# Attention and a Mish feed-forward on one core: the order of the seven-product blocks, attention by single tiles, PSUM banks as tiles of their own, sums on GpSimd

## The chip, the cores and the metric

The kernel runs on one core of a Trainium2 chip. The metric is the device time in microseconds (us), median of the runs shown. TensorE multiplies matrices into PSUM, VectorE and ScalarE read PSUM and work elementwise, GpSimd works on SBUF, SyncE issues transfers. Each engine takes its instructions in the order in which the program wrote them and waits on semaphores.

## What is computed

Attention inside chunks of 64 positions, then a feed-forward with Mish, all in float32:

```python
q_c = q.reshape(B, H, nc, chunk, D)          # B 8, H 8, S 576, chunk 64, D 64; k_c, v_c alike
scores = scale * np.matmul(q_c, k_c.transpose(0, 1, 2, 4, 3))
scores = scores - np.max(scores, axis=-1, keepdims=True)
attn = np.exp(scores)
attn = attn / (np.sum(attn, axis=-1, keepdims=True) + 1e-09)
out = np.matmul(attn, v_c)
...
x = np.ascontiguousarray(attn_out.transpose(0, 2, 1, 3)).reshape(B * S, H * D)   # 4608 x 512
h = x @ w_in                                  # 512 x 2048
sp = np.where(h > 20.0, h, np.log1p(np.exp(np.minimum(h, 20.0))))
g = h * np.tanh(sp)
return (g @ w_out).astype(np.float32)         # 2048 x 512
```

## The kernel before, in words

**Tiles.** The 4608 tokens are 36 attention tiles of 128 tokens (two chunks of 64). Every factor of the feed-forward is split into two parts of fewer bits, a rounded one and the residue ("hi" and "lo"), and a product is the sum of three matmuls: lo by hi, hi by lo, hi by hi. ScalarE writes the hi part (a cast), VectorE the lo part (a subtraction of two SBUF operands).

**First part: plain blocks.** Two blocks of 512 tokens (tiles 0 to 7) run in 32 "slots" (`slot(s)`), one for each block and each 128 columns of `w_in`: `up` of the next slot (12 matmuls), `down` of the last (12 matmuls into four accumulators `o_o`), the attention of tiles 4 to 7, and of tiles 8 to 15 (`AHEAD`, pairs 4 to 7), and the preparation of the weights. In slots 16 to 31 the weights of the second part are made: `t_sum` (two sums of 512 columns), `t_diff` (four differences of 256), `t_hi`, `t_lo`, once in two slots, and written to DRAM (`dwi`). After slot 31 come the down of the last slot and the store of the second block.

**Second part: seven-product blocks.** Tiles 8 to 35 are four blocks of seven tiles (896 tokens, in halves of 448 columns). The up projection is a two-by-two block product with seven products in place of eight (Strassen's, in Winograd's form), for pairs of 128 columns of `w_in`. Eight such pairs make eight "sets" for each block, 32 in all (set z is pair z mod 8 of block z div 8). In a set TensorE runs

- `s_up(z, k)`, k = 0 to 6 ("u0" to "u6"), six matmuls of 448 columns each. u0, u3, u5 and u6 accumulate in a bank `al` of that set, u1 in the first half of the tile `bg`, u2 and u4 in the second half. `s_copy` (ScalarE) keeps intermediate states p1 (after u0), p5 (after u2) and u2 (after u3). `s_c` (VectorE) adds them to the products: c11 after u1, c12 after u4, c22 after u5. `s_hi` (ScalarE: Mish and cast) and `s_lo` (VectorE) make g of the four quadrants 11, 12, 22 and 21 from them.
- `s_down(z-1, i)`, i = 0 to 6 ("d0" to "d6"), six matmuls of 512 columns each with the g of the set before, for the seven tiles of tokens. They alternate between the two halves (banks) of one tile `d`. `s_out` empties each: a copy on ScalarE in a block's first set, then a sum on VectorE into `sum0` to `sum6`, in the last set into a new tile `ob` (of three) that two transfers write to DRAM.

**Order.** The order of the second part is written by hand: `ORDER` gives fourteen places of a set, alternately u and d, with d5 and d6 next to each other and u6 last. `when(z, m, ...)` puts work of the other engines behind place m of set z, `pe[z, m]` work of TensorE.

**Attention in the second part.** `plan_pair` puts a pair of tiles into a set: scores at place 1, maximum and subtraction at 2, exponential at 4, sums and reciprocals at 5, normalisation at 7, transposes at 9, values at 12, the copy into x at 13. Ten pairs (8 to 17) have three, four and three sets of the first three blocks. `ps_a` is a tile of two banks for scores, transposes and values. With it PSUM is full: two banks in `ps_h`, two in `ps_a`, four in `ps_o`.

**x of the next block.** In a block's last set (z = 7, 15, 23) `plan_x` makes the seven operands `xo0` to `xo6` of the next block: four sums or differences of 896 elements (`x_sum`: xs and x, L553), seven casts (`x_hi`, ScalarE, L558), seven residues (`x_lo`, VectorE, L561), each behind the product that last reads its place. For the first block they are made before and after slot 30.

Line numbers in the profile of before: `up` L308, `down` L346, `store` L360 and L362, small matmuls of attention L180, transposes L251, `s_up` L602, `s_down` L621, `s_out` L646 (copy) and L649 (sum), `s_copy` L660, `s_c` L669, `s_hi` L681 (Mish) and L682 (cast), `s_lo` L685. A program line that stands for several helper calls keeps the helper's number.

Of the kernel before, what the change touches and what calls it, by code (L numbers as in the profile page):

```python
# [25 lines left out]
def kernel(  # L26
# [485 lines left out]
    cols = {}  # L512
    rows = [[] for _ in range(NSB)]
    for j in range(FIRST_TILE // 2, NPAIR):
        blocks = [(2 * j + t - FIRST_TILE) // BT for t in range(2)]
        parts = [(blocks[0], BOTH)] if blocks[0] == blocks[1] else [(blocks[t], slice(t, t + 1)) for t in range(2)]
        cols[j] = []
        for b, ts in parts:
            cols[j].append((b, len(rows[b]) * CHUNK, ts))
            rows[b] += [((2 * j + t) * 2 + c) * CHUNK for c in range(2) for t in range(ts.start, ts.stop)]  # L520
# [39 lines left out]
    def x_lo(b, k):  # L560
        nc.vector.tensor_tensor(  # L561
# [79 lines left out]
    def s_out(z, i):  # L641
        b, s = divmod(z, NS)
        o = places["d"][:, (BT * z + i) % 2]
# [289 lines left out]
```

## Time and profile before

| | us |
|---|---|
| median of 3 runs (lowest, highest) | 981.82 (980.07, 983.72) |
| the profiled execution itself | 984.02 |
| its span, first to last instruction | 982.2 |
| TensorE busy / VectorE / ScalarE / GpSimd in the span | 875.6 / 532.1 / 426.0 / 0.7 |
| mean granted TensorE clock | 0.974 |

A row of the timeline reads: start, duration, engine, line, operation, out<-in, partitions x elements, type, count; in brackets the idle time of that engine just before, and who released it. PE is TensorE's matmuls, PEld its loads of the stationary operand, DVE VectorE, ACT ScalarE, POOL GpSimd. A group's row has the busy time, the mean ns of one, and behind the second bar the idle time before the group with its main releaser. The first part lasts to about 225 us, set 0 to about 252, the last set's downs begin at 961.

### The profile page before, as it was taken

To read this page: it belongs to the slowest core of one execution; us is meant where nothing else is said; L and a number is where in the kernel's file an instruction comes from. 1 tells how busy PE (TensorE), PEld (TensorE's weight loads), DVE (VectorE), ACT (ScalarE), POOL (GpSimd) and SP (SyncE) were. 2 spreads that over 40 slices of the span, in tenths; PEclk is the share of its full clock that TensorE was granted. 3 is DMA by queue.
4 is the path that set the end of the run, shared out by engine and by line. 5 is a ranking of instruction groups with operands and counts; after the bars stand their busy time and mean duration, and the time that the engine had idled before them with its cause. 6 is when DMAs were issued, how large, how long until landed. Compare 5 with 4: busy or idle time off the path is not lost.

```text
span 982.2 us, 14424 instructions
## 1 busy us (share of the span) xinstructions
PE 875.6 (89%) x5984; PEld 719.2 (73%) x5984; DVE 532.1 (54%) x802; ACT 426.0 (43%) x669; POOL 0.7 (0%) x6
## 2 busy tenths in 40 slices
...
GB/s 258 253 324 369 307 220 158 139 100 263 211 175 143 171 174 148 85 215 225 150 174 115 227 113 43 220 183 196 91 234 133 129 60 229 129 129 160 183 43 75
DMA packets 51297, 170.81 MB, mean 174 GB/s; under 512 B 5152, under 2 KB 11296, under 8 KB 39968
## 3 DMA queue, kind: packets, MB, share of 16 engines
...
q10 hardware_dynamic: 848, 1.44, 0.4%
...
## 4 chain that ended last, share of the span: by engine, by line
PE 64%; DVE 16%; ACT 9%; DMA 5%; issue 5%; SPq 1%; POOLq 0%; DVEq 0%; ACTq 0%; POOL 0%
PE d L621 28%; PE al L602 14%; PE bg L602 8%; PE o_o L346 4%; PE h L308 3%; DVE sum L649 3%; DMA wos<-in_w_out 2%; DVE xo L561 2%; PE s L180 2%; DMA out<-ob 2%; DVE m L207 2%; PE av L180 2%; DVE c L669 2%; PE pt L251 2%; ACT c L681 1%
## 5 line engine op out<-in xcount | busy, mean ns | idle before, releaser
L621 PE MATMUL d<-wo,g 128*128 128x512 f32 x1344 | 362.1, 405 | 76.8 <-DVE sum L649 57.2
L621 PEld LDWEIGHTS d<-wo,g 128*128 128x128 f32 x1344 | 252.0, 191 | 148.9 <-DVE sum L649 74.5
L649 DVE TENSOR_TENSOR sum<-d,sum 128x512 f32<-128x512 f32 x168 | 115.6, 688 | 141.8 <-PE d L621 141.7
L602 PE MATMUL al<-xo,ring 128*128 128x448 f32 x768 | 179.2, 376 | 1.9 <-DVE c L669 1.9
L602 PEld LDWEIGHTS al<-xo,ring 128*128 128x128 f32 x768 | 148.4, 195 | 19.7 <-DVE c L669 2.3
L681 ACT ACTIVATE c<-c 128x448 f32<-128x448 f32 x96 | 55.5, 578 | 232.3 <-DVE c L669 232.2
L602 PE MATMUL bg<-xo,ring 128*128 128x448 f32 x576 | 137.4, 375 | 7.5 <-DVE c L669 7.5
L685 DVE TENSOR_TENSOR g<-c,g 128x448 fp32r<-128x448 f32 x128 | 79.3, 620 | 91.4 <-ACT g L682 91.4
L602 PEld LDWEIGHTS bg<-xo,ring 128*128 128x128 f32 x576 | 108.6, 191 | 25.5 <-DVE c L669 12.1
L308 PE MATMUL h<-x,w 128*128 128x512 f32 (+1 forms) x396 | 94.6, 389 | 0.8 <-ACT x L282 0.8
L308 PEld LDWEIGHTS h<-x,w 128*128 128x128 f32 x396 | 73.6, 192 | 15.8 <-ACT x L282 0.9
L346 PE MATMUL o_o<-w,gh 128*128 128x512 f32 x256 | 81.8, 402 | 0.0
L682 ACT CAST g<-c 128x448 fp32r<-128x448 f32 x128 | 72.5, 567 | 4.1
L346 PE MATMUL o_o<-w,gl 128*128 128x512 f32 x128 | 53.1, 415 | 6.1 <-DVE gl L333 6.1
L346 PEld LDWEIGHTS o_o<-w,gh 128*128 128x128 f32 x256 | 49.8, 195 | 10.3
L681 ACT ACTIVATE c<-al 128x448 f32<-128x448 f32 x32 | 17.4, 545 | 82.8 <-PE al L602 82.8
L561 DVE TENSOR_TENSOR xo<-x,xo 128x896 fp32r<-128x896 f32 x24 | 25.9, 1091 | 37.7 <-ACT xo L558 37.7
L660 ACT COPY u<-al 128x448 f32<-128x448 f32 x32 | 17.1, 534 | 57.2 <-PE al L602 57.0
L649 DVE TENSOR_TENSOR ob<-d,sum 128x512 f32<-128x512 f32 x28 | 19.3, 690 | 36.1 <-PE d L621 26.7
L669 DVE TENSOR_TENSOR c<-bg,u 128x448 f32<-128x448 f32 x32 | 20.0, 624 | 32.0 <-PE bg L602 32.0
L207 DVE TENSOR_REDUCE m<-s 128x16 f32<-128x1024 f32 (+1 forms) x20 | 22.3, 1117 | 23.5 <-PE s L180 23.4
L346 PEld LDWEIGHTS o_o<-w,gl 128*128 128x128 f32 x128 | 24.7, 193 | 12.7 <-DVE gl L333 7.5
...
## 6 DMA issues: line engine op xcount, KB each, us to landing
...
```

The lines of the kernel that those rows point to most:

```text
L180: nc.tensor.matmul(o[h * CHUNK : (h + 1) * CHUNK, c, t - ts.start, g], lhsT=l[rows, t, 2 * g + h], rhs=r[rows, t, 2 * g + h], start=True, ...
L207: nc.vector.tensor_reduce(out=small(j, "m", t), in_=st[j]["s", t.start].rearrange("p c t g k -> p c (t g) k"), op=ALU.max, axis=AX.X,)
L308: nc.tensor.matmul(h[:, cols], lhsT=wi(f, w_, kt), rhs=x[:, kt, cols], start=(n == 0), stop=(n == 3 * NK - 1),)
L346: nc.tensor.matmul(acc[t], lhsT=g[:, sl], rhs=w_part(f, w_), start=(f == 0 and n == 0), stop=(f == NF - 1 and n == 2),)
L561: nc.vector.tensor_tensor(out=xo[k][:, 1], in0=x_src(b, k), in1=raw(xo[k][:, 0]), op=ALU.subtract)
L602: nc.tensor.matmul(o[:, :HALF], lhsT=w_[:, wn, kt * P : (kt + 1) * P], rhs=x[:, xn, kt], start=(n == 0 and k < 3), stop=(n == 5), skip_gro ...
L621: nc.tensor.matmul(o, lhsT=g_tile(z, e)[:, gn, i * P : (i + 1) * P], rhs=wos[z % 2][:, e, wn], start=(n == 0), stop=(n == 5),)
L649: nc.vector.tensor_tensor(out=to, in0=o, in1=a, op=ALU.add)
L669: nc.vector.tensor_tensor(out=ct[z, n], in0=o[:, :HALF], in1=ct.pop((z, other)), op=ALU.add)
L681: nc.scalar.activation(out=ct[z, n], in_=src, func=AF.Mish)
L682: nc.scalar.copy(out=g_view(z, n, 0), in_=ct[z, n])
L685: nc.vector.tensor_tensor(out=g_view(z, n, 1), in0=ct.pop((z, n)), in1=raw(g_view(z, n, 0)), op=ALU.subtract)
```

## The change

- `ORDER` becomes u0, e6, u1, d0, u2, d1, ..., u6, d5: u and d strictly alternate. d0 to d5 are of the set before, e6 is d6 of the set two before. Two more rounds of `s_set` behind set 31 run the remaining downs.
- PSUM: after set 0 the pool of the first part is closed, and its four banks become four tiles `b`, `g`, `d0`, `d1`. u1 writes `b`, u2 and u4 write `g`, the downs alternate between `d0` and `d1`, and those of set 31 go round all four. In set 0, b and g are a tile of `ps_a`.
- Attention in the second part is planned by single tiles (`plan_tile`), one in each of the sets 1 to 6, 8 to 14 and 16 to 22: twenty in place of ten pairs. Scores, maximum and v at place 1, subtraction at 3, exponential at 4, sums at 7, normalisation at 8, transposes at 9, values at 13, the copy into x at place 0 of the next set. Columns of x follow tiles (`x_put`, `row`).
- Sums: `t_sum` and `t_diff` run on GpSimd; so do `x_sum` for blocks 1 to 3, and their residue `x_lo` of k = 2. The residues of k = 4, 5, 6 move to the next set, and `x_hi` from the even places to the odd ones behind them.
- `s_out` of a block's last set adds in the sum's own tile and writes it out from there.
- Passage to the second part: the downs of slots 30 and 31 are divided and lie at places 1, 3, 5 and 11 of set 0; residues and casts of the first x are spread differently; the ring of weights is loaded after slot 27.

The diff, cut:

```diff
-    ps_o = ctx.enter_context(tc.tile_pool(name="ps_o", bufs=1, space=bass.MemoryType.PSUM))
+    plain = ctx.enter_context(ExitStack())
+    ps_o = plain.enter_context(tc.tile_pool(name="ps_o", bufs=1, space=bass.MemoryType.PSUM))
...
-            nc.vector.tensor_tensor(
+            nc.gpsimd.tensor_tensor(
                 out=d[e], in0=raw(w_part(f, 0)), in1=raw(w_part(f, 1)), op=ALU.add
             )
...
-            nc.vector.tensor_tensor(out=o, in0=a, in1=b, op=ALU.subtract)
+            nc.gpsimd.tensor_tensor(out=o, in0=a, in1=b, op=ALU.subtract)
...
+    def n_scores(n):
+        qk = tl[n]["qk"]
+        small_mm(n_bank(n, "s"), qk[:, 0:1], qk[:, 1:2], slice(0, 1))
...
+    LOW_BY_POOL = (2,)
...
-        nc.vector.tensor_tensor(out=o, in0=l, in1=r, op=op)
+        engine = nc.gpsimd if b else nc.vector
+        engine.tensor_tensor(out=o, in0=l, in1=r, op=op)
...
     def x_lo(b, k):
-        nc.vector.tensor_tensor(
+        engine = nc.gpsimd if b and k in LOW_BY_POOL else nc.vector
+        engine.tensor_tensor(
...
-            places["bg"] = ps_o.tile([P, 2, DM], F32, name="bg", tag="o0")
+            o = ps_a.tile([P, 2, DM], F32, name="bg", tag="a")
+            places["b"], places["g"] = o[:, 0], o[:, 1]
...
-        o = places["bg"][:, int(k > 1)] if k in (1, 2, 4) else places["a", z]
+        o = places["b"] if k == 1 else places["g"] if k in (2, 4) else places["a", z]
...
+    def d_bank(z, i):
+        if z == NSB * NS - 1:
+            return places[("d0", "d1", "b", "g")[(BT * z + i) % 4]]
+        return places[f"d{(BT * z + i) % 2}"]
...
-        o = places["d"][:, (BT * z + i) % 2]
+        o = d_bank(z, i)
         a = s_sum(i)
...
-        to = a if s < NS - 1 else wst.tile([P, DM], F32, name=f"ob_{z}_{i}", tag="c")
-        nc.vector.tensor_tensor(out=to, in0=o, in1=a, op=ALU.add)
+        nc.vector.tensor_tensor(out=a, in0=o, in1=a, op=ALU.add)
...
-        if 1 <= s <= N:
+        if 1 <= s < N - 1:
             down(s - 1)
...
-    ORDER = (("u", 0), ("d", 0), ("u", 1), ("d", 1), ("u", 2), ("d", 2), ("u", 3), ("d", 3),
-             ("u", 4), ("d", 4), ("u", 5), ("d", 5), ("d", 6), ("u", 6))
+    ORDER = (("u", 0), ("e", 6), ("u", 1), ("d", 0), ("u", 2), ("d", 1), ("u", 3), ("d", 2),
+             ("u", 4), ("d", 3), ("u", 5), ("d", 4), ("u", 6), ("d", 5))
...
-        when(z, 13, lambda: s_hi(z, 21))
-        when(z + 1, 0, lambda: s_lo(z, 21))
...
+        when(z, 12, lambda: s_hi(z, 21))
+        when(z, 13, lambda: s_lo(z, 21))
...
-        when(z - 1, 13, lambda: x_sum(b, 2))
-        for k, m in enumerate((0, 2, 4, 6, 8, 10, 13)):
-            when(z, m, lambda k=k: x_hi(b, k), lambda k=k: x_lo(b, k))
-        when(z, 2, lambda: x_sum(b, 5), lambda: x_sum(b, 3))
+        for k in range(7):
+            when(z, 2 * k + 1, lambda k=k: x_hi(b, k))
+        for k, m in enumerate((1, 3, 5, 6)):
+            when(z, m + (k == 3), lambda k=k: x_lo(b, k))
+        for k, m in (4, 1), (5, 3), (6, 6):
+            when(z + 1, m, lambda k=k: x_lo(b, k))
+        when(z, 0, lambda: x_sum(b, 2))
+        when(z, 2, lambda: x_sum(b, 5))
+        when(z, 2, lambda: x_sum(b, 3))
         when(z, 4, lambda: x_sum(b, 4))
...
+    def plan_tile(z, n):
+        when(z - 1, 2, lambda: n_load(n))
+        pe[z, 1] = lambda: n_scores(n)
+        when(z, 1, lambda: n_load_v(n), lambda: n_max(n))
+        when(z, 3, lambda: n_sub(n))
+        when(z, 4, lambda: n_exp(n))
+        when(z, 7, lambda: n_inverse(n))
+        when(z, 8, lambda: n_norm(n))
+        pe[z, 9] = lambda: n_transpose(n)
+        when(z, 10, lambda: n_copy(n))
+        pe[z, 13] = lambda: n_values(n)
+        when(z + 1, 0, lambda: n_x(n))
...
+            back = {"u": 0, "d": 1, "e": 2}[kind]
             if kind == "u":
-                s_up(z, i)
-            elif z > 0:
-                s_down(z - 1, i)
...
+                if z < NSB * NS:
+                    s_up(z, i)
+            elif 0 <= z - back < NSB * NS:
+                s_down(z - back, i)
             if (z, m) in pe:
                 pe[z, m]()
+            if kind != "u" and 0 <= z - back < NSB * NS:
+                s_out(z - back, i)
...
+        pe[0, 1] = lambda: down(N - 2, (0, 1))
+        pe[0, 3] = lambda: down(N - 2, (2, 3))
+        pe[0, 5] = lambda: down(N - 1, (0, 1))
+        pe[0, 11] = lambda: down(N - 1, (2, 3))
+        for m, i in (4, 2), (5, 4), (6, 7):
+            when(0, i, lambda m=m: x_lo(0, m))
...
+        s_set(0)
+        plain.close()
+        ps_s = ctx.enter_context(tc.tile_pool(name="ps_s", bufs=1, space=bass.MemoryType.PSUM))
+        for n in "b", "g", "d0", "d1":
+            places[n] = ps_s.tile([P, DM], F32, name=n, tag=n)
+        for z in range(1, ZN + 2):
             s_set(z)
```

Three places where rows moved. The first is the end of set 30 and the start of set 31 on TensorE. `al`, `bg`, `b`, `g` are outputs of up products, `d` and `d_...` of downs, each down in two rows of three. Before:

```order
L602 MATMUL bg<-xo_2442,ring_2455 128x448 x6
L621 MATMUL d<-wo_2599,g_2660 128x512 x3
L621 MATMUL d<-wo_2599,g_2717 128x512 x3
L602 MATMUL al_7130<-xo_2445,ring_2455 128x448 x6
L621 MATMUL d<-wo_2599,g_2660 128x512 x3
L621 MATMUL d<-wo_2599,g_2717 128x512 x3
L621 MATMUL d<-wo_2599,g_2660 128x512 x3
L621 MATMUL d<-wo_2599,g_2717 128x512 x3
L602 MATMUL al_7130<-xo_2448,ring_2451 128x448 x6
L602 MATMUL al_7249<-xo_2387,ring_2451 128x448 x6
L621 MATMUL d<-wo_2490,g_2532 128x512 x3
L621 MATMUL d<-wo_2490,g_2567 128x512 x3
```

Of the change:

```order
L685 MATMUL al_7292<-xo_2455,ring_2263 128x448 x6
L707 MATMUL d_2600<-wo_2632,g_2643 128x512 x3
L707 MATMUL d_2600<-wo_2632,g_2705 128x512 x3
L685 MATMUL al_7292<-xo_2457,ring_2261 128x448 x6
L707 MATMUL d_2599<-wo_2632,g_2643 128x512 x3
L707 MATMUL d_2599<-wo_2632,g_2705 128x512 x3
L685 MATMUL al_7411<-xo_2396,ring_2261 128x448 x6
L707 MATMUL d_2600<-wo_2632,g_2643 128x512 x3
L707 MATMUL d_2600<-wo_2632,g_2705 128x512 x3
L685 MATMUL b<-xo_2401,ring_2261 128x448 x6
L707 MATMUL d_2599<-wo_2488,g_2501 128x512 x3
L707 MATMUL d_2599<-wo_2488,g_2555 128x512 x3
```

The two downs next to each other and the two ups next to each other are gone; a down stands between the last up that writes `al_7292` and the one before it, where two stood.

The second is VectorE in set 7, which prepares x of block 1 (`xo` residues, `xs` and `x` sums). Before, from the second product's rounding on:

```order
L561 TENSOR_TENSOR xo_2390<-x_1_2541,xo_2390 128x896
L553 TENSOR_TENSOR x_1_2541<-x_1_2541 128x2x448
L553 TENSOR_TENSOR x_1_2541<-xs_3595,x_1_2541 128x2x448
L649 TENSOR_TENSOR sum_2643<-d,sum_2643 128x512
L685 TENSOR_TENSOR g_2660<-c_7_3623,g_2660 128x448
L561 TENSOR_TENSOR xo_2395<-xs_3595,xo_2395 128x896
L553 TENSOR_TENSOR x_1_2541<-x_1_2541 128x2x448
L649 TENSOR_TENSOR sum_2689<-d,sum_2689 128x512
```

Of the change, on VectorE:

```order
L643 TENSOR_TENSOR xo_2401<-x_1_2448,xo_2401 128x896
L734 TENSOR_TENSOR sum_2654<-d_2600,sum_2654 128x512
L734 TENSOR_TENSOR sum_2688<-d_2599,sum_2688 128x512
L643 TENSOR_TENSOR xo_2450<-x_1_2448,xo_2450 128x896
L758 TENSOR_TENSOR c_7_3741<-g,u_7_3724 128x448
L734 TENSOR_TENSOR sum_2688<-d_2600,sum_2688 128x512
L774 TENSOR_TENSOR g_2705<-c_7_3741,g_2705 128x448
L758 TENSOR_TENSOR c_7_3760<-al_3652,p_7_3706 128x448
```

and on GpSimd:

```order
L634 TENSOR_TENSOR xs_3662<-x_1_2448 128x896
L634 TENSOR_TENSOR x_1_2448<-x_1_2448 128x2x448
L634 TENSOR_TENSOR x_1_2448<-xs_3662,x_1_2448 128x2x448
L634 TENSOR_TENSOR x_1_2448<-x_1_2448 128x2x448
L643 TENSOR_TENSOR xo_2404<-xs_3662,xo_2404 128x896
```

The sums that stood between VectorE's `sum` rows are now five rows of GpSimd.

The third is VectorE in set 6 of the change, which has an attention tile, from the sum of d2 on:

```order
L734 TENSOR_TENSOR sum_2688<-d_2600,sum_2688 128x512
L580 TENSOR_REDUCE r_3569<-vp_3513 128x8
L581 TENSOR_SCALAR r_3569<-r_3569 128x8
L582 RECIPROCAL r_3569<-r_3569 128x8
L586 TENSOR_TENSOR vp_3513<-vp_3513,r_3569 128x512
L758 TENSOR_TENSOR c_6_3580<-g,u_6_3560 128x448
L734 TENSOR_TENSOR sum_2688<-d_2599,sum_2688 128x512
L774 TENSOR_TENSOR g_2555<-c_6_3580,g_2555 128x448
L758 TENSOR_TENSOR c_6_3606<-al_3479,p_6_3545 128x448
```

Before, in a set with a pair (set 5), the same stretch read:

```order
L235 TENSOR_REDUCE r_0_3356<-p_3325 128x8x2
L236 TENSOR_SCALAR r_0_3356<-r_0_3356 128x16
L237 RECIPROCAL r_0_3356<-r_0_3356 128x16
L649 TENSOR_TENSOR sum_2689<-d,sum_2689 128x512
L242 TENSOR_TENSOR p_3325<-p_3325,r_0_3356 128x2x8x64
L649 TENSOR_TENSOR sum_2689<-d,sum_2689 128x512
L669 TENSOR_TENSOR c_5_3384<-bg,u_5_3367 128x448
L649 TENSOR_TENSOR sum_2734<-d,sum_2734 128x512
L685 TENSOR_TENSOR g_2717<-c_5_3384,g_2717 128x448
```

A sum stood between the reciprocals and the normalisation, and another between the normalisation and c12 (`c_5_3384`); now both parts of attention stand together ahead of c12 (`c_6_3580`).

More of the change, by code (lines that the diff above doesn't have):

```diff
@@ L352, in down, with store @@
                 )
-    def store(b):
-        for t in range(TOK // P):
+    def store(b, ts=range(4)):
+        for t in ts:
             o = wst.tile([P, DM, 2], U32, name=f"ob_{b}_{t}", tag="st", bufs=4)
@@ L509, in t_lo @@
                 nc.sync.dma_start(out=raw(dwi_of(s, k)), in_=raw(o[:, e]))
[L512 to L520, printed above, removed]
@@ new lines, in row, with n_load, n_load_v @@
+    def row(b, u):
+        c, t = divmod(u, BT)
+        return ((FIRST_TILE + b * BT + t) * 2 + c) * CHUNK
+    tl = {}
+    def n_load(n):
+        qk = at.tile([P, 2, H, CHUNK], F32, name=f"qk_{n}", tag="A")
+        nc.sync.dma_start(out=qk[:, 0], in_=q[n])
+        nc.sync.dma_start(out=qk[:, 1], in_=k[n])
+        tl[n] = {"qk": qk}
+    def n_load_v(n):
+        d = tl[n]
+        vp = at.tile([P, 2, H, CHUNK], F32, name=f"vp_{n}", tag="A")
+        nc.sync.dma_start(out=vp[:, 0], in_=v[n])
+        d["v"] = vp[:, 0:1]
+        d["p"] = vp[:, 1].rearrange("p (g c) k -> p g c k", c=2)
@@ new lines, in n_bank, with n_max, n_sub @@
+    def n_bank(n, name):
+        o = ps_a.tile([P, 2, 2, NG, CHUNK], F32, name=f"n{name}_{n}", tag="a")
+        tl[n][name] = o[:, :, 0]
+        return o[:, :, 0:1]
+    def n_scores(n):
+        qk = tl[n]["qk"]
+        small_mm(n_bank(n, "s"), qk[:, 0:1], qk[:, 1:2], slice(0, 1))
+    def n_max(n):
+        d = tl[n]
+        d["m"] = sm_p.tile([P, 2, NG], F32, name=f"m_{n}", tag="m")
+        nc.vector.tensor_reduce(out=d["m"], in_=d["s"], op=ALU.max, axis=AX.X)
+    def n_sub(n):
+        d = tl[n]
+        nc.vector.tensor_tensor(
+            out=d["p"].rearrange("p g c k -> p c g k"),
+            in0=d["s"],
+            in1=d["m"].unsqueeze(3).broadcast_to([P, 2, NG, CHUNK]),
+            op=ALU.subtract,
+        )
@@ new lines, in n_exp, with n_inverse, n_norm @@
+    def n_exp(n):
+        p = tl[n]["p"]
+        nc.scalar.activation(out=p, in_=p, func=AF.Exp, scale=SCALE)
+    def n_inverse(n):
+        d = tl[n]
+        d["r"] = r = sm_p.tile([P, NG, 2], F32, name=f"r_{n}", tag="r")
+        nc.vector.tensor_reduce(out=r, in_=d["p"], op=ALU.add, axis=AX.X)
+        nc.vector.tensor_scalar(out=r, in0=r, scalar1=1e-9, scalar2=None, op0=ALU.add)
+        nc.vector.reciprocal(out=r, in_=r)
+    def n_norm(n):
+        d = tl[n]
+        nc.vector.tensor_tensor(
+            out=d["p"], in0=d["p"], in1=d["r"].unsqueeze(3).broadcast_to([P, NG, 2, CHUNK]), op=ALU.mult
+        )
```

121 lines of the change are left out of this document (61 added, 60 removed).

## The prediction

> **What bounds the kernel now.** I read the page first (shares, chain, costliest groups), then the timeline of TensorE in the second part, where a "set" is seven up products u0 to u6 and seven down groups d0 to d6.
>
> ```profile
> span 982.2 us, 14424 instructions
> L621 PE MATMUL d<-wo,g 128*128 128x512 f32 x1344 | 362.1, 405 | 76.8 <-DVE sum L649 57.2
> ```
>
> The largest idle time of TensorE stands before the down matmuls, released by VectorE's sum that empties their bank. The timeline shows where. The twelve-matmul rows (u6 and the next u0) mark the sets.
>
> ```profile
> 340.88 2.60 PE L602 MATMUL al<-xo,ring 128*128 128x448 f32 x12
> ...
> 349.09 1.48 PE L602 MATMUL bg<-xo,ring 128*128 128x448 f32 x6 [0.36 <-DVE c L669]
> ...
> 354.97 1.67 PE L621 MATMUL d<-wo,g 128*128 128x512 f32 x6 [1.79 <-DVE sum L649]
> ...
> 363.50 1.67 PE L621 MATMUL d<-wo,g 128*128 128x512 f32 x6 [0.79 <-DVE sum L649]
> ...
> 366.20 2.74 PE L602 MATMUL al<-xo,ring 128*128 128x448 f32 x12
> 368.78 1.56 PE L621 MATMUL d<-wo,g 128*128 128x512 f32 x6
> ...
> 371.40 1.56 PE L621 MATMUL d<-wo,g 128*128 128x512 f32 x6
> ...
> 384.21 1.66 PE L621 MATMUL d<-wo,g 128*128 128x512 f32 x6 [0.78 <-DVE sum L649]
> 385.71 2.60 PE L602 MATMUL al<-xo,ring 128*128 128x448 f32 x12
> ```
>
> A set with attention takes 366.20 - 340.88 = 25.32 us, a plain one 385.71 - 366.20 = 19.51. Where u and d alternate without a wait, a pair takes 371.40 - 368.78 = 2.62, so seven take 18.34. A plain set is longer by the wait of d6, which follows d5 with no up product between them: 0.78 until the sum of d5 is done, although d6 writes the other bank. So one tile with two banks is waited for as a whole. The attention set has that wait, one of 1.79 (VectorE normalises two tiles ahead of the sum) and one of 0.36 at u2 for the reader of the other half of `bg`.
>
> Three sets prepare the next block's x, and cost most:
>
> ```profile
> 397.94 2.82 PE L621 MATMUL d<-wo,g 128*128 128x512 f32 x6 [3.58 <-DVE sum L649]
> ...
> 409.89 1.65 PE L621 MATMUL d<-wo,g 128*128 128x512 f32 x6 [1.44 <-DVE sum L649]
> 414.73 2.59 PE L621 MATMUL d<-wo,g 128*128 128x512 f32 x6 [3.19 <-DVE sum L649]
> 417.12 3.29 PE L602 MATMUL al<-xo,ring 128*128 128x448 f32 x12
> ```
> ```profile
> 403.83 1.09 DVE L561 TENSOR_TENSOR xo<-x,xo 128x896 fp32r<-128x896 f32 x1 [2.33 <-ACT xo L558]
> ```
>
> This set takes 417.12 - 385.71 = 31.41. VectorE does eleven operations of 1.09 there, and queues each residue behind ScalarE's rounding of the same place, with the sum behind both. Six matmuls after such a wait take 2.82 instead of 1.67: the clock has fallen too. The set after it can wait for a transfer:
>
> ```profile
> 632.11 2.93 PE L621 MATMUL d<-wo,g 128*128 128x512 f32 x6 [4.98 <-DVE ob L649]
> ```
> ```profile
> 631.36 0.69 DVE L649 TENSOR_TENSOR ob<-d,sum 128x512 f32<-128x512 f32 x1 [4.95 <-DMA out<-ob]
> ```
>
> **The change, part by part.**
>
> *Sets.* From u6 of set 0 (252.22, below) to u6 of set 31 (960.17, below) are 31 sets and 707.95 us. With d6 moved behind the next u0, every d has an up product before it, and a d needs only the sum two groups back: 2.62 + 1.22 of slack against a sum of 0.69. I take 31 x 18.34 = 568.5. The first of these sets has no d5 and d6 of a predecessor: 2 x 1.40 less, that is 2.8 (a d is 2.62 - 1.22, with 1.22 for a u from 960.17 to 961.39).
>
> *Attention by tiles.* A pair costs 25.32 - 18.34 - (0.36 + 1.79 + 0.79) = 4.04 of TensorE itself. A part of it is paid per call:
>
> ```profile
> 344.79 1.02 PEld L180 LDWEIGHTS s<-k,q 64*64 64x64 f32 x64 [0.36 <-issue]
> ```
>
> This pause precedes the scores; I count the same before the values: 0.72 that isn't halved. A single tile costs (4.04 - 0.72) / 2 + 0.72 = 2.38, and twenty tiles 47.6 where ten pairs took 40.4. New is what VectorE has ahead of c12. After the change u6 (which overwrites what c22 reads) comes one d after u5, formerly two. The chain from the end of u4 is c12, Mish, rounding, residue, c22:
>
> ```profile
> L669 DVE TENSOR_TENSOR c<-bg,u 128x448 f32<-128x448 f32 x32 | 20.0, 624 | 32.0 <-PE bg L602 32.0
> L681 ACT ACTIVATE c<-c 128x448 f32<-128x448 f32 x96 | 55.5, 578 | 232.3 <-DVE c L669 232.2
> L682 ACT CAST g<-c 128x448 fp32r<-128x448 f32 x128 | 72.5, 567 | 4.1
> L685 DVE TENSOR_TENSOR g<-c,g 128x448 fp32r<-128x448 f32 x128 | 79.3, 620 | 91.4 <-ACT g L682 91.4
> L235 DVE TENSOR_REDUCE r<-p 128x16 f32<-128x1024 f32 x16 | 19.5, 1221 | 16.9 <-ACT p L230 16.7
> L237 DVE RECIPROCAL r<-r 128x16 f32<-128x16 f32 x16 | 4.1, 253 | 0.6
> ```
>
> 0.62 + 0.58 + 0.57 + 0.62 + 0.62 = 3.0, with hand-overs about 3.5; the room is d3 + u5 + d4 = 4.0, in attention sets 4.5 with four transposes. So plain sets don't wait. In attention sets the sum of d2 (0.69), half a reduction (0.61), two small operations (0.25 and one no longer, 0.4 by estimate) and a normalisation of as many elements as the reduction (0.61) stand ahead of c12: 2.3 from the end of d2, 1.1 past the end of u4, where 1.0 is free. I take 0.3 per tile, 20 x 0.3 = 6.0 (bounds 0 and 1.6, see the first rival).
>
> *The x sets.* VectorE keeps three residues of 1.09 there; three go to the next set, one and four sums to GpSimd. VectorE then has 7 x 0.69 + 7 x 0.62 + 3.3 = 12.4 of 18.3. No row shows GpSimd in such a sum. The nearest is
>
> ```profile
> masks.py:199 POOL TENSOR_SCALAR_AFFINE_SELECT ident<-ident 128x128 f32<-128x128 f32 x1 | 0.3, 292 | 0.1
> ```
>
> 0.292 for 128 elements, by length 2.04 for 896 and 1.17 for 512. Lower end VectorE's 1.09, upper end 4.1 if each of two inputs costs a pass; I take 2.04. Four sums in a row are 8.2, ready for the rounding of x4 at 4.5 x 2.62 = 11.8. I leave 1.2 per set for rounding and residues that still meet the chain: 3.6 (bounds 0 and 13). Output from the sum's own tile, rewritten a set later, takes the output wait away.
>
> So the stretch is 568.5 - 2.8 + 47.6 + 6.0 + 3.6 = 622.9: **85.0 saved**.
>
> *The passage into set 0.*
>
> ```profile
> 224.50 0.61 PE L346 MATMUL o_o<-w,gh 128*128 128x512 f32 x2
> 228.58 0.80 PE L346 MATMUL o_o<-w,gl 128*128 128x512 f32 x1 [3.46 <-DVE gl L333]
> 229.17 1.05 PE L346 MATMUL o_o<-w,gh 128*128 128x512 f32 x2
> ...
> 243.54 1.83 PE L602 MATMUL bg<-xo,ring 128*128 128x448 f32 x6 [3.51 <-DVE c L669]
> ...
> 252.22 2.74 PE L602 MATMUL al<-xo,ring 128*128 128x448 f32 x12 [1.95 <-DVE c L669]
> ```
> ```profile
> 227.83 0.69 DVE L333 TENSOR_TENSOR gl<-z,gh 128x512 fp32r<-128x512 f32 x1
> ...
> 242.27 0.69 DVE L360 COPY ob<-o_o 128x512 f32<-128x512 f32 x1 [3.78 <-DMA dwi<-ts]
> ```
>
> Before, 225.1 to 252.22 is 27.1. After: six u of 1.22 (7.3), 24 down matmuls of 1.40 / 6 (5.6), a wait for gl at 228.5 of which u0 covers 1.2 (2.2), u2 behind c11 (1.0), u6 behind c22 (0.8): 16.9. That saves 10.2. Whether 2.2 of idleness lowers the clock is open: 1.79 didn't (354.97), 3.19 did (414.73). Cold, two matmuls took 1.05 in place of 0.61, so twelve cost 2.6 more; I take half, **8.9 saved**. The Trainium skill, "TensorE: Matmul & The Clock Gate", Part 1, puts the idle window at about 3.4 us; the trace's cold rows after 3.19 and 3.46 lie about there. By the page the 1.3 would not be charged, and the sum would be 883.
>
> *The weight sums.* Slots of the first part are matmuls end to end: 48 x 0.233 = 11.2 for two slots. Moved off VectorE they save nothing on TensorE; on GpSimd they take 4 x 1.17 = 4.7 per two slots and lie beside it (bounds 2.7 and 9.4): 0.
>
> *The end.*
>
> ```profile
> 960.17 1.38 PE L602 MATMUL al<-xo,ring 128*128 128x448 f32 x6
> 961.39 1.54 PE L621 MATMUL d<-wo,g 128*128 128x512 f32 x6
> 964.05 1.65 PE L621 MATMUL d<-wo,g 128*128 128x512 f32 x6 [1.12 <-DVE ob L649]
> ...
> 976.28 1.66 PE L621 MATMUL d<-wo,g 128*128 128x512 f32 x6 [0.78 <-DVE ob L649]
> ```
>
> The last downs come every (976.28 - 964.05) / 5 = 2.45, again one tile; own tiles and four banks let them come every 1.40. After u6 there are now nine (two of set 30): 12.6, and 982.2 - 977.9 = 4.3 behind the last, 16.9 against 20.8: **3.9 saved**.
>
> Sum: 85.0 + 8.9 + 3.9 = 97.8. The profiled execution took 984.02, 1.8 more than its span: 886.2 is left. It lies 2.2 above the median 981.82 of the runs, so I forecast **884**.
>
> **The rivals.**
>
> *Attention in front of the chain (0.10).*
>
> ```profile
> 350.27 1.28 ACT L230 ACT_TABLE_LOAD   x1
> ```
>
> ScalarE loads a table on each change between Mish and the exponential. If the Mish table isn't reloaded in the shadow of the wait for c12, its load joins the chain: 1.28 + 0.3 a tile, 32 in place of 6, **910**. For it: ScalarE's order has the exponential in each of 20 sets, formerly 10. Against: the load needs no data and stands ahead of the waiting Mish.
>
> *GpSimd holds VectorE (0.10).* Residues read two SBUF operands, as GpSimd's sums do. Were each held for one sum, the x sets would carry 12.4 + 5 x 2.04 = 22.6 on VectorE, 4.3 over TensorE's 18.3, 13 for three, and eight pairs of weight slots a late residue of about 1.2: 884 - 3.6 + 13 + 10 = **903**. The rows of before can't show it, since GpSimd is idle beside VectorE. The Trainium skill, "SBUF — State Buffer", "Who interferes with whom", says so outright: a VectorE instruction with two SBUF inputs and a GpSimd instruction that reads SBUF exclude each other. No run here shows it yet.
>
> *The tiles don't part (0.05).* If the waits come from something other than the shared tile, alternation still hides them, but the end keeps 9 x 1.05 and u2 its 0.36 in 20 sets: **901**.
>
> *GpSimd becomes the bound (0.03), slower than before.* With its sums k times my price, two weight slots take 4.7k against 11.2, and four sums of an x set 8.2k against 11.8: eight times the one and three times the other are 62k - 125 once both are exceeded. From k = 3.6 (4.2 us for 512 elements, six times VectorE's) the whole gain is gone; at k = 4.5, **1039**. Against: 292 ns for 128 elements. The Trainium skill, "GPSIMD Engine Reference", 3.1, gives 4497 ns for an add of 2048, an estimate of 1.1 for 512; by that k is 1.
>
> **How the numbers follow.** The forecast has 0.72, with its own range 868 (no waits of attention or x, pairs of 2.60 as in the rows below in place of 2.62, and a warm passage) to 897 (the x sets at their upper bound).
>
> ```profile
> 324.10 1.54 PE L621 MATMUL d<-wo,g 128*128 128x512 f32 x6
> ...
> 326.70 1.54 PE L621 MATMUL d<-wo,g 128*128 128x512 f32 x6
> ```
>
> The range takes in the rivals up to 910: 866 to 910; what is left out is the fourth and the tails. A measurement of this kernel tells about 0.5% from no change. Faster 0.96, within 0.5% 0.01, slower 0.03.
>
> **What would show it.** Twelve-matmul rows vanish; plain sets stand 18.3 apart, attention sets 21, x sets under 20; no d waits for a sum; the last nine downs stand 1.4 apart. Waits of `al` for c22 would show the first rival, VectorE residues longer than 0.62 or 1.09 the second, ScalarE or VectorE released by POOL with TensorE idle the fourth. Sets above 19 without attention would make me wrong.

## The result, and the profile after

| | before | after |
|---|---|---|
| median (lowest, highest), us | 980.95 (977.43, 983.72) | 872.36 (871.29, 875.1) |
| the profiled execution, us | 984.02 | 871.29 |
| its span | 982.2 | 869.5 |
| TensorE / VectorE / ScalarE / GpSimd busy | 875.6 / 532.1 / 426.0 / 0.7 | 845.2 / 516.9 / 452.9 / 84.0 |
| granted TensorE clock | 0.974 | 0.997 |

Time after to time before is 0.8899, with a 95% interval of 0.8862 to 0.8936: 11% faster. The prediction was 884, range 866 to 910.

From the page of the changed kernel, three groups (busy time and mean ns behind the first bar, idle time ahead of the group behind the second):

```profile
L707 PE MATMUL d<-wo,g 128*128 128x512 f32 x1320 | 339.4, 393 | 0.0
...
L334 DVE TENSOR_TENSOR gl<-z,gh 128x512 fp32r<-128x512 f32 x32 | 26.4, 824 | 12.8 <-ACT gh L327 12.3
L643 DVE TENSOR_TENSOR xo<-x,xo 128x896 fp32r<-128x896 f32 x24 | 33.8, 1410 | 0.0
```

The 76.8 us that TensorE idled ahead of the down matmuls are gone. The two VectorE groups are what the change made worse: a residue of 896 elements takes 1.41 on average where it took 1.09 before, and gl of 512 takes 0.82 where it took 0.69.

The timeline of TensorE, by stage: u1 (tile `b`) of two attention sets and of two plain ones, the x set of block 1, the passage, the end.

```profile
224.58 1.37 PE L685 MATMUL al<-xo,ring 128*128 128x448 f32 x6
229.16 0.60 PE L347 MATMUL o_o<-w,gl 128*128 128x512 f32 x1 [3.21 <-DVE gl L334]
229.56 1.05 PE L347 MATMUL o_o<-w,gh 128*128 128x512 f32 x2
...
243.18 2.08 PE L685 MATMUL al<-xo,ring 128*128 128x448 f32 x9 [0.59 <-DVE c L758]
...
287.20 1.49 PE L685 MATMUL b<-xo,ring 128*128 128x448 f32 x6
...
307.71 1.49 PE L685 MATMUL b<-xo,ring 128*128 128x448 f32 x6
...
368.55 1.38 PE L685 MATMUL b<-xo,ring 128*128 128x448 f32 x6
...
381.99 1.49 PE L685 MATMUL al<-xo,ring 128*128 128x448 f32 x6 [0.32 <-DVE c L758]
...
387.98 1.49 PE L685 MATMUL b<-xo,ring 128*128 128x448 f32 x6
...
766.03 1.38 PE L685 MATMUL b<-xo,ring 128*128 128x448 f32 x6
...
784.19 1.38 PE L685 MATMUL b<-xo,ring 128*128 128x448 f32 x6
...
851.61 1.38 PE L685 MATMUL al<-xo,ring 128*128 128x448 f32 x6
852.83 4.26 PE L707 MATMUL d<-wo,g 128*128 128x512 f32 x18
...
863.73 1.52 PE L707 MATMUL g<-wo,g 128*128 128x512 f32 x6
```

A plain set takes 784.19 - 766.03 = 18.16, an attention set 307.71 - 287.20 = 20.51, the x set 387.98 - 368.55 = 19.43 (from u1 to u1, so with the scores of the tile of set 8; from u0 to u0 it is 18.81); no down waits. From u6 of set 0 (243.18) to u6 of set 31 (851.61) are 608.4 us where 707.95 were: 99.5 saved. Set 0 starts its u6 9.0 earlier than before (252.22), and behind u6 of set 31 the end takes 17.9 instead of 22.0, 4.1 saved. Together 112.7, the difference of the two profiled executions. The medians differ by 108.6, since the profiled execution before lies above every run in the table, and the one after is the fastest of its kernel.

### The profile page after: what moved, and what is told of

Same layout as the page of the kernel before. It is cut to its first block, busy times and chain, and to the rows that moved or that the text cites. A ratio compares the mean times of both kernels' runs of the same rounds, so it can differ in the third digit from the quotient of the medians.

```text
span 869.5 us, 14677 instructions
## 1 busy us (share of the span) xinstructions
PE 845.2 (97%) x5984; PEld 708.9 (82%) x5984; DVE 516.9 (59%) x799; ACT 452.9 (52%) x721; POOL 84.0 (10%) x69
## 4 chain that ended last, share of the span: by engine, by line
PE 87%; DVE 9%; issue 2%; ACT 2%; DMA 0%; POOL 0%; DVEq 0%; ACTq 0%; POOLq 0%; SPq 0%
PE d L707 34%; PE al L685 18%; PE g L685 8%; PE o_o L347 8%; PE h L309 6%; PE b L685 5%; PE ns L181 1%; PE nav L181 1%; PE npt L595 1%; PE s L181 1%; DVE p L243 1%; PE pt L252 1%; DVE gl L334 1%; DVE r L236 1%; DVE xo L643 1%
## 5 line engine op out<-in xcount | busy, mean ns | idle before, releaser
L707 PE MATMUL d<-wo,g 128*128 128x512 f32 x1320 | 339.4, 393 | 0.0
L734 DVE TENSOR_TENSOR sum<-d,sum 128x512 f32<-128x512 f32 x192 | 132.5, 690 | 183.0 <-PE d L707 180.9
L685 PEld LDWEIGHTS al<-xo,ring 128*128 128x128 f32 x768 | 141.0, 188 | 18.8 <-DVE c L758 3.3
L685 PE MATMUL g<-xo,ring 128*128 128x448 f32 x372 | 85.3, 365 | 0.0
L685 PEld LDWEIGHTS g<-xo,ring 128*128 128x128 f32 x372 | 69.9, 188 | 8.6
L634 POOL TENSOR_TENSOR xs<-x 128x896 f32<-128x896 f32 x3 | 6.4, 2123 | 437.4 <-ACT x L524 437.4
L685 PE MATMUL b<-xo,ring 128*128 128x448 f32 x186 | 44.8, 377 | 0.0
L685 PEld LDWEIGHTS b<-xo,ring 128*128 128x128 f32 x186 | 33.4, 188 | 4.1
L334 DVE TENSOR_TENSOR gl<-z,gh 128x512 fp32r<-128x512 f32 x32 | 26.4, 824 | 12.8 <-ACT gh L327 12.3
L643 DVE TENSOR_TENSOR xo<-x,xo 128x896 fp32r<-128x896 f32 x24 | 33.8, 1410 | 0.0
L347 PEld LDWEIGHTS o_o<-w,gl 128*128 128x128 f32 x128 | 24.2, 189 | 11.3 <-DVE gl L334 6.4
```

The source lines that it names most:

```text
L334: nc.vector.tensor_tensor(out=d["gl"], in0=d["z"], in1=d["gh"].bitcast(F32), op=ALU.subtract)
L347: nc.tensor.matmul(acc[t], lhsT=g[:, sl], rhs=w_part(f, w_), start=(f == 0 and n == 0), stop=(f == NF - 1 and n == 2),)
L643: engine.tensor_tensor(out=xo[k][:, 1], in0=x_src(b, k), in1=raw(xo[k][:, 0]), op=ALU.subtract)
L685: nc.tensor.matmul(o[:, :HALF], lhsT=w_[:, wn, kt * P : (kt + 1) * P], rhs=x[:, xn, kt], start=(n == 0 and k < 3), stop=(n == 5), skip_gro ...
L707: nc.tensor.matmul(o, lhsT=g_tile(z, e)[:, gn, i * P : (i + 1) * P], rhs=wos[z % 2][:, e, wn], start=(n == 0), stop=(n == 5),)
L734: nc.vector.tensor_tensor(out=a, in0=o, in1=a, op=ALU.add)
```

## The experiments

Each expectation names its theories; their letters hold for the runs of one part. All medians stand beside the kernel before on the same chip: 980.15 in the first four runs, 978.94 in the next four, 982.08 in the last four. The three groups ran on different chips, so across groups the ratios are the fairer comparison. The code cuts leave lines out at "...".

### Which edit removed the waits: tiles or order

**own_only**: the kernel before with four tiles, its own order, attention by pairs and everything else kept.

```diff
...
 elif m == 1:
     down(N - 1)
     store(NB - 1)
+    plain.close()
+    ps_s = ctx.enter_context(tc.tile_pool(name="ps_s", bufs=1, space=bass.MemoryType.PSUM))
+    for n in "b", "g", "d0", "d1":
+        places[n] = ps_s.tile([P, DM], F32, name=n, tag=n)
...
```

> The kernel before with one edit: b, g, d0 and d1 as four tiles after the down of slot 31, in place of the two tiles bg and d. Theory A (a tile of two banks is waited for as a whole, so a down waits for the sum of the group just before it, not of the group two back): of the 76.8 us that TensorE waited ahead of the downs, 10 to 15 remain (x sets, where VectorE is late by more than one group), and the 0.36 ahead of u2 goes: 912 to 925. Theory B (the downs wait because VectorE's queue is late, and the tile does not matter): 975 to 982.

**shared_alt**: the changed kernel, with halves of two tiles in place of four tiles.

```diff
-for n in "b", "g", "d0", "d1":
-    places[n] = ps_s.tile([P, DM], F32, name=n, tag=n)
+for n in ("b", "g"), ("d0", "d1"):
+    o = ps_s.tile([P, 2, DM], F32, name=n[0] + n[1], tag=n[0])
+    places[n[0]], places[n[1]] = o[:, 0], o[:, 1]
```

> The changed kernel with b,g as halves of one tile and d0,d1 as halves of another. Theory A: alternation hides the sum of the group before (0.7 to 0.9 against an up product of 1.22) in plain sets, but u2 waits 0.36 in 20 sets (7 us), the last downs wait about 1.05 each (9), and x sets wait where a lengthened residue stands ahead of a sum (0 to 9): 888 to 898. Theory C (the order alone made the gain, the tiles nothing): 872 to 875.

**adj_own**: the changed kernel with d6 directly behind d5 (place 13), nothing at place 1.

```diff
-back = {"u": 0, "d": 1, "e": 2}[kind]
+back = {"u": 0, "d": 1, "e": 99}[kind]
...
+if m == 13 and z > 0:
+    s_down(z - 1, 6)
+    s_out(z - 1, 6)
...
```

> The changed kernel with d6 directly behind d5 of the same set, own tiles kept. Theory A: d6 needs only the sum of d4, which is long done: 871 to 875. Theory C (alternation itself is what removes the wait of d6): 0.78 in 31 sets, 24 more, 896.

**adj_shared**: both edits.

> The changed kernel with both undone: d6 behind d5, and b,g and d0,d1 as halves. Theory A: the cost of shared halves under alternation plus 0.78 for d6 in 31 sets, 24 above the run with shared halves alone: 912 to 922. Theory C: as with own tiles and d6 behind d5, 896.

Measured:

| | median, us | ratio to before, 95% interval |
|---|---|---|
| own_only | 887.17 | 0.9058, 0.9029 to 0.9087 |
| shared_alt | 885.84 | 0.9031, 0.8992 to 0.9071 |
| adj_own | 874.92 | 0.8932, 0.8903 to 0.8962 |
| adj_shared | 903.22 | 0.9214, 0.9181 to 0.9247 |

The four tiles alone bring 93 of the 109 us. Theory B (VectorE's queue is late, the tile does not matter) and theory C (the order made it) fall. With own tiles d6 may stand behind d5: 874.92, so the order is worth about 2.4 at the medians, which the intervals do not tell from nothing. With shared halves it may not. Both runs with halves came out lower than expected: u2 waits in the x sets alone, and in attention sets the values' matmuls stand between d5 and d6 and cover the wait but for 0.16. u1 of adjacent plain sets in adj_own, then u2 of adjacent plain sets with a d6 between them in adj_shared:

```profile
770.01 1.38 PE L685 MATMUL b<-xo,ring 128*128 128x448 f32 x6
...
788.14 1.38 PE L685 MATMUL b<-xo,ring 128*128 128x448 f32 x6
```
```profile
770.04 1.54 PE L707 MATMUL d0d<-wo,g 128*128 128x512 f32 x6
771.41 1.38 PE L685 MATMUL bg<-xo,ring 128*128 128x448 f32 x6
772.63 1.54 PE L707 MATMUL d0d<-wo,g 128*128 128x512 f32 x6
...
785.33 1.67 PE L707 MATMUL d0d<-wo,g 128*128 128x512 f32 x6 [0.79 <-DVE sum L734]
...
790.63 1.38 PE L685 MATMUL bg<-xo,ring 128*128 128x448 f32 x6
```

18.13 against 19.22: 1.09 more, although the wait shown is 0.79. The rest, about 0.3, does not stand in brackets; I read it as the overlap that a group behind a wait loses. Its own row is 1.67 where the others' are 1.54 (0.13), and the row before it could not overlap with it (a row of 1.54 is otherwise followed after 1.37, 0.17). With alternation and shared halves, in shared_alt, a pair of u and d is longer too:

```profile
755.01 1.56 PE L707 MATMUL d0d<-wo,g 128*128 128x512 f32 x6
...
757.63 1.56 PE L707 MATMUL d0d<-wo,g 128*128 128x512 f32 x6
```

No wait is shown, and yet a pair takes 2.62, so a plain set 18.34, the very number that the prediction took from before; with own tiles it is 2.59. The halves by themselves do not explain these 0.03. adj_shared has halves too, and its pairs without a wait take 772.63 - 770.04 = 2.59; the attention sets of shared_alt take 20.5, as in the changed kernel; and in the kernel before, most pairs without a wait take 2.59 or 2.60. Where the 0.03 come from stays open.

That a wait costs more than its idle time is also why own_only came out 25 to 38 below what I expected of it. The engines' busy time and the group of the downs on its page, and two attention sets of its timeline:

```profile
PE 843.8 (95%) x5984; PEld 713.1 (80%) x5984; DVE 529.2 (60%) x802; ACT 423.9 (48%) x669; POOL 0.7 (0%) x6
...
L618 PE MATMUL d<-wo,g 128*128 128x512 f32 x1344 | 343.0, 394 | 13.1 <-DVE sum L646 11.0
```
```profile
297.34 1.49 PE L601 MATMUL b<-xo,ring 128*128 128x448 f32 x6
...
337.17 1.49 PE L601 MATMUL b<-xo,ring 128*128 128x448 f32 x6
```

I had counted only the idle time (76.8 to 13.1, that is 63.7). TensorE's busy time for the same 5984 matmuls fell as well, from 875.6 to 843.8: a down matmul went from 405 to 394 ns, and the granted clock rose from 0.974 to 0.989. Together 95.6 of span.

The remaining parts overlap with the tiles. adj_shared has neither tiles nor alternation, and still stands 77 below before. In its trace the downs wait 15.7 in all, nearly as little as in own_only. Its plain sets take 19.2, no less than those of the kernel before; its x sets take 21.7 in place of 31.4. I read this as shorter work on VectorE (single tiles, spread residues), which makes the sums earlier and so removes waits that own tiles also remove; no run tries these parts alone on the kernel before. The gains do not add: brought in first, the tiles are worth 93, brought in last, 28 (903.22 to 874.92).

### Attention by tiles: a loss that the rest hides

In own_only a pair of attention sets takes 337.17 - 297.34 = 39.83, that is 3.57 for a pair of tiles over two sets of 18.13. In the changed kernel a single tile costs 20.51 - 18.16 = 2.35, a pair of them 4.70.

**pairs**: the changed kernel with ten pairs.

```diff
-if s < BT and n < NT and n >= 2 * (AHEAD[-1] + 1):
-    plan_tile(z, n)
+if z in PAIR_OF:
+    plan_pair(z, PAIR_OF[z])
...
+PAIR_OF = dict(zip((1, 3, 5, 8, 10, 12, 14, 17, 19, 21), range(8, 18)))
+def plan_pair(z, j):
+    when(z - 1, 2, lambda: load_qk(j))
+    pe[z, 1] = lambda: a_scores(j)
+    when(z, 1, lambda: load_v(j), lambda: a_max(j))
+    when(z, 3, lambda: a_sub(j))
+    when(z, 4, lambda: a_exp(j))
+    when(z, 5, lambda: a_inverse(j))
+    when(z, 7, lambda: a_norm(j))
+    pe[z, 9] = lambda: a_transpose(j)
+    when(z, 10, lambda: a_copy(j))
+    pe[z, 13] = lambda: a_values(j)
+    when(z + 1, 0, lambda: a_x(j, 0), lambda: a_x(j, 1))
```

> The changed kernel with attention again by ten pairs (sets 1, 3, 5, 8, 10, 12, 14, 17, 19, 21): scores at place 1, subtraction 3, exponential 4, sums 5, normalisation 7, transposes 9, values 13. In the run with own banks alone a pair cost 20.51 + 19.32 - 2 x 18.13 = 3.57 of TensorE, in the changed kernel a single tile 20.51 - 18.15 = 2.36. Theory A (single tiles are a loss that the other parts hide, 10 x (4.72 - 3.57) = 11.5): 859 to 863. Theory B (single tiles are needed so that VectorE is in time for c12 and c22; with a pair u6 waits 1 to 2 in ten sets): 871 to 881, with waits of al for c in those sets.

Measured: 865.69 us (864.29 to 867.15), ratio 0.8832, interval 0.8809 to 0.8855, 6.8 below the 872.51 of the changed kernel in the last rounds, by the ratios 5.7. Theory A holds in its sign, not in its whole size (859 to 863 expected); theory B falls. Its timeline of TensorE, a pair in an ordinary set, and the pair in set 8, where the last residues of an x set lie beside it:

```profile
289.05 1.49 PE L685 MATMUL b<-xo,ring 128*128 128x448 f32 x6
...
329.12 1.49 PE L685 MATMUL b<-xo,ring 128*128 128x448 f32 x6
...
388.34 1.49 PE L685 MATMUL b<-xo,ring 128*128 128x448 f32 x6
...
401.04 1.06 PE L252 MATMUL pt<-ident,p 128*128 128x128 f32 x8 [1.23 <-DVE p L243]
...
410.98 1.38 PE L685 MATMUL b<-xo,ring 128*128 128x448 f32 x6
```

A pair costs 40.07 - 2 x 18.15 = 3.77, so ten save 9.3; set 8 gives about 2 of it back (410.98 - 388.34 = 22.64, with waits of 1.23 and 0.57). c22 keeps no u6 waiting in any pair's set.

### The x sets: where the operations lie matters more than who does them

**x_on_vector**: sums and the residue of k = 2 on VectorE, at the changed places. **x_old**: that, with each cast and its residue at the even places again and none in the next set, nearly as before.

```diff
-engine = nc.gpsimd if b else nc.vector
+engine = nc.vector
...
-LOW_BY_POOL = (2,)
+LOW_BY_POOL = ()
```
```diff
...
+for k in range(7):
+    when(z, 2 * k, lambda k=k: x_hi(b, k), lambda k=k: x_lo(b, k))
...
```

> The changed kernel with the x sums and the residue of k = 2 on VectorE, all places kept. Theory A (GpSimd relieves VectorE of five operations of 1.09 in an x set): VectorE then has 17.9 of work in 18.2, and waits of 2 to 5 us come up in each of three x sets: 878 to 888. Theory B (GpSimd's sums lengthen VectorE's residues beside them by as much as they relieve): 869 to 873, and residues of 1.09 in place of the mean of 1.41.

> The changed kernel with the x sets as before: sums and residues on VectorE, each cast and its residue at the even place behind the product that reads it, none in the next set. Theory A (spreading the residues over two sets is what took the waits out of the x sets): an x set is 3 to 5 us longer than the 19.4 of the changed kernel, 882 to 888. Theory B (own banks and alternation alone absorb it): 873 to 876, as with the sums on VectorE at the changed places.

Measured: x_on_vector 875.0 (872.15 to 877.22), ratio 0.8928, interval 0.8899 to 0.8956; x_old 888.07 (886.63 to 890.08), ratio 0.9043, interval 0.9018 to 0.9068. The x set in x_on_vector, then in x_old:

```profile
373.12 1.38 PE L685 MATMUL b<-xo,ring 128*128 128x448 f32 x6
...
393.14 1.49 PE L685 MATMUL b<-xo,ring 128*128 128x448 f32 x6
```
```profile
370.68 1.38 PE L685 MATMUL b<-xo,ring 128*128 128x448 f32 x6
...
379.11 1.65 PE L707 MATMUL d<-wo,g 128*128 128x512 f32 x6 [1.87 <-DVE sum L734]
...
389.23 1.50 PE L685 MATMUL al<-xo,ring 128*128 128x448 f32 x6 [2.74 <-DVE c L758]
...
395.28 1.49 PE L685 MATMUL b<-xo,ring 128*128 128x448 f32 x6
```

20.02 and 24.60, where the changed kernel has 19.43. GpSimd saves 0.6 per x set, 1.7 over the three; the medians show 2.5, which their intervals do not tell from nothing. Theory A had expected 6 to 16, though VectorE carries 17.9 us of work in that set by my count. The places bring 4.6 per set, 13.7 over the three, and the medians 13.1: theory A there. This edit moves casts by a place and takes three residues out of the set; which of the two counts for how much was not tried.

In x_on_vector a residue of 896 takes 1.13 on average, in the changed kernel 1.41:

```profile
L643 DVE TENSOR_TENSOR xo<-x,xo 128x896 fp32r<-128x896 f32 x24 | 27.1, 1128 | 0.0
```

### The weight sums on GpSimd: not free

**w_on_vector** has all weight sums on VectorE again, **w_last_pool** all but the last pair of slots; **after_again** is the changed kernel. The edit of w_last_pool, which the four differences of `t_diff` share:

```diff
...
-nc.gpsimd.tensor_tensor(
+(nc.gpsimd if s == NS - 1 else nc.vector).tensor_tensor(
     out=d[e], in0=raw(w_part(f, 0)), in1=raw(w_part(f, 1)), op=ALU.add
...
```

> The changed kernel with the weight sums back on VectorE. Theory A (the first part is bound by TensorE, and the sums lie beside it on either engine): 870.5 to 873, TensorE's first part ending at 224 to 226. Theory B (VectorE was late there): 876 to 885. In both, the gl of 512 elements takes 0.69 everywhere, where beside GpSimd its mean was 0.82.

> The changed kernel with the weight sums on VectorE in all pairs of slots but the last (there GpSimd has them, as changed). Theory A (GpSimd beside VectorE lengthens its casts and residues in the first part, so that p of three attention pairs comes late for the transposes, 1.34, 0.81 and the waits ahead of scores): the first part is 2 to 5 us shorter, 868 to 870.5. Theory B (the sums lie beside TensorE's work on either engine, price nothing): as the unaltered kernel within 1, with the same waits ahead of the transposes.

> The changed kernel, unaltered, so that the other three stand beside it in the same rounds: 870 to 875. No theory differs on it.

Measured: w_on_vector 870.63 (868.85 to 871.87), ratio 0.8883, interval 0.8858 to 0.8909. The other two ran in the same rounds: after_again 872.51 (871.56 to 875.6), 0.889, interval 0.887 to 0.8911, and w_last_pool 870.14 (868.4 to 871.08), 0.8858, interval 0.8838 to 0.8879. Their medians differ by 2.4, and the intervals just overlap. The traces are clearer. The up products of slots 14 and 30 (16 slots apart) start here in the changed kernel, then in w_last_pool:

```profile
112.68 2.88 PE L309 MATMUL h<-x,w 128*128 128x512 f32 x12
...
219.14 2.88 PE L309 MATMUL h<-x,w 128*128 128x512 f32 x12
```
```profile
115.28 2.88 PE L309 MATMUL h<-x,w 128*128 128x512 f32 x12
...
218.90 2.88 PE L309 MATMUL h<-x,w 128*128 128x512 f32 x12
```

106.46 against 103.62. Over all traces of this study the stretch is 102.7 to 103.6 in the five kernels with these sums on VectorE, all or but the last (before among them, 103.61), and 105.4 to 108.7 in the nine with GpSimd. From slot 16 to slot 30 the five take 90.5 and the nine 91.7 to 92.2, so 1.2 to 1.7 of the price lie there. The rest, which varies, lies in slots 14 and 15: in the changed kernel TensorE pauses there for 2.13 ahead of scores, in w_last_pool for 0.90. In after_again the pause is 1.84, and the up product behind it takes 4.61 in place of 3.0. VectorE in the changed kernel, GpSimd beside it, and VectorE in w_last_pool:

```profile
149.37 0.96 DVE L329 CAST gh<-z 128x512 fp32r<-128x512 f32 x1
...
151.40 1.21 DVE L236 TENSOR_REDUCE r<-p 128x16 f32<-128x1024 f32 x1
152.64 1.28 DVE L237 TENSOR_SCALAR r<-r 128x16 f32<-128x16 f32 x1
```
```profile
149.30 0.74 POOL L493 TENSOR_TENSOR t<-c 128x256 f32<-128x256 f32 x1
...
150.89 3.00 POOL L479 TENSOR_TENSOR c<-w 128x512 f32<-128x512 f32 x2
```
```profile
150.70 0.42 DVE L329 CAST gh<-z 128x512 fp32r<-128x512 f32 x1
...
153.16 0.18 DVE L237 TENSOR_SCALAR r<-r 128x16 f32<-128x16 f32 x1
```

The operation on 16 elements takes 1.28 instead of 0.18, and ends (153.92) as GpSimd's sums do (153.89): by this row VectorE is held until GpSimd's instruction is over. The normalisation behind it is late, and TensorE waits for it, in the changed kernel and in w_last_pool:

```profile
156.63 1.07 PE L252 MATMUL pt<-ident,p 128*128 128x128 f32 x8 [1.34 <-DVE p L243]
```
```profile
156.90 1.07 PE L252 MATMUL pt<-ident,p 128*128 128x128 f32 x8 [0.28 <-DVE p L243]
```

### The passage

**gl_early**: in the changed kernel the residues 1 and 2 of the first x go behind gl of slot 30, its last sum and later residues into set 0, the last weight residues behind c22.

```diff
 if s == N - 3:
     ...
+    x_hi(0, 1)
+    x_hi(0, 2)
 if s == N - 2:
     a_x(AHEAD[-1], 1)
+    x_lo(0, 1)
     x_hi(0, 3)
+    x_lo(0, 2)
...
+when(0, 3, lambda: x_lo(0, 3), lambda: x_sum(0, 4), lambda: x_hi(0, 4))
+when(0, 4, lambda: x_lo(0, 4))
+when(0, 7, lambda: x_hi(0, 5), lambda: x_lo(0, 5), lambda: x_hi(0, 6))
+when(0, 9, lambda: x_lo(0, 6))
...
+when(0, 10, lambda: t_hi(NS - 1), lambda: t_lo(NS - 1))
```

> The changed kernel with the first x's residues 1 and 2 and its last sum behind the gl of slot 30, later ones spread over set 0, and the last weight residues behind c22 of set 0. Theory A (the gap of 3.21 in the passage is VectorE's queue ahead of gl of slot 30, and the cold clock behind it comes from the gap): the gap goes, and u6 of set 0 starts at 238 to 240 in place of 243.18: 867 to 869. Theory B (VectorE's work in the passage, 16 us without a pause, is the bound, and the wait returns at u2 or u6): 871 to 873.

Measured: 871.55 (868.74 to 873.16), ratio 0.8891, interval 0.8863 to 0.8919, not to be told from the changed kernel, so the time lies in theory B's range. The mechanism of theory A is seen in the trace alone:

```profile
230.88 0.50 PE L347 MATMUL o_o<-w,gl 128*128 128x512 f32 x1 [0.20 <-DVE gl L334]
...
244.62 2.66 PE L685 MATMUL al<-xo,ring 128*128 128x448 f32 x12 [1.01 <-DVE c L758]
```

The wait for gl is 0.20, no cold rows follow, u6 waits 1.01 where it waited 0.59, and u0 to u6 of set 0 take 244.62 - 229.31 = 15.3 where the changed kernel has 243.18 - 224.58 = 18.6. But u0 starts 4.7 later in that execution. Of this 3.4 lie ahead of the edit (the up of slot 14 starts at 116.09, in the changed kernel at 112.68), and another 1.3 in the slots with GpSimd's sums (107.8 against 106.5); why the start came out so stays open.

### What the findings give together

**best**: pairs, weight sums on VectorE but for the last, gl_early, and the residue of k = 6 at place 9 of the next set.

> Pairs, weight sums on VectorE but for the last, the residues of the first x spread round gl of slot 30, and the residue of k = 6 at place 9 of the set. If the gains add: 872.4 - 6.7 (pairs) - 1.2 (the two waits of set 8) - 2 to 4 (weight sums) - 3 (passage): 857 to 861. If the passage or the first part only shifts its wait: 863 to 866.

Measured: 861.2 us (857.7 to 865.05), ratio 0.8774, interval 0.8748 to 0.88: 11.3 below the changed kernel in the same rounds, at the upper edge of the 857 to 861 expected if the gains add. Its passage:

```profile
220.52 1.37 PE L685 MATMUL al<-xo,ring 128*128 128x448 f32 x6
...
235.83 2.67 PE L685 MATMUL al<-xo,ring 128*128 128x448 f32 x12 [1.00 <-DVE c L758]
```

Again 15.3 from u0 to u6.

## Why the prediction was right, and where not

- **The cause** held: a tile of two banks is waited for as a whole, and own tiles part them (own_only). Credit for it was misplaced in part: the prediction let the 0.78 of a plain set go "with d6 moved behind the next u0". The tiles alone do that (plain sets of 18.13 in own_only and adj_own); the move adds 2.4 at the medians, within their noise.
- **Pitch of a set**, 18.34 predicted, 18.15 measured: mis-sized by 31 x 0.19 = 5.9. The pair of 2.62 that it came from was one of two kinds: the prediction also shows one of 326.70 - 324.10 = 2.60 and kept that for its lower end. What makes a pair 2.62 stays open (shared_alt against adj_shared).
- **Attention**: 2.38 per tile predicted, 2.35 measured. The 0.3 per tile for the chain to c22 did not appear, 6.0 too many. That tiles cost more than pairs was seen (47.6 against 40.4). But a pair costs 3.57 with own tiles, not 4.04, most likely because the 4.04 still held what groups behind waits lose; so the loss is larger than priced. The 2.38 is in part luck: with 3.57 the same sum would have given 2.15.
- **The x sets**: 1.2 each predicted, 3.6 in all. Measured from u0 to u0 they take 18.81, 18.87 and 18.90, about 0.7 above a plain set, 2.1 in all, with waits of 0.32 to 0.36 for c22.
- The stretch was thus 608.4 instead of 622.9, 14.5 of the 14.9 by which the 97.8 forecast fell short of the 112.7 measured. The forecast lay 11.6 above the median; of the conditions that its lower end of 868 named, the pairs and the tiles without waits came about, the warm passage did not.
- **The passage**: u6 of set 0 starts 9.0 earlier, 8.9 predicted, yet not by its parts, so the agreement is luck. Counted from the up of slot 30 the passage takes 243.18 - 219.14 = 24.0 where it took 32.7, 8.7 less; an early start and the weight sums (below) nearly cancel in the rest. The gap before gl was 3.21 where I had 2.2, as gl ran at 228.42 and not at 227.83, behind sums and residues of up to 1.63 in place of 1.09, and u0 began at 224.58 and not at 225.1. Cold rows did follow, at a granted clock of 0.57 from 229 to 233. By the Trainium skill, "TensorE: Matmul & The Clock Gate", Part 1, a gap of 3.21 would lie just under the idle window of about 3.4 us. The rows of 1.05 show it as cold, so the row decides.
- **The end**: 4.1 saved, 3.9 predicted, downs 1.36 apart where I had 1.40.
- **The weight sums**, 0 predicted, cost about 2.4: VectorE was not beside the path there but just ahead of it. In the profiled pair this was hidden by a start that came 3.2 earlier (up of slot 14 at 112.68, before at 115.90), which is luck: over the fourteen traces that start lies anywhere between 111.99 and 116.09.
- **Rivals.** No al waited for c22 in an attention set (the first). The second's mechanism is real, at a price of 2.4 in the weight slots, while in the x sets GpSimd still saves 0.6 each: the rival stood 19 above the forecast for both. There VectorE has idle time, and I take it that TensorE therefore does not see the hold. The third, with shared halves, would have been 885.84, where I computed 901, 17 above the forecast; it lies 13.5 above the measured time. GpSimd's 512 elements took 1.34, k = 1.15, far from the 3.6 at which the fourth begins.
